# Attention and gated feed-forward on one core: the planner of the attention phase gets other lengths and urgencies, and the instruction order follows

## The chip, the cores and the metric

The kernel runs on one core of one Trainium2 chip. The metric is the device time of one execution in microseconds (us). Three runs of the kernel before gave 1236.25, 1241.36 and 1247.63; their median, 1241.36 us, is the time before.

## What is computed

The reference runs a random-feature attention over 8 batches, 8 heads, 576 tokens and 64 dimensions (128 features), and sends its output through an RMS norm and a gated feed-forward layer:

```
h   = (x*scale) @ omega.T - |x*scale|^2/2         # for q and for k
phi = exp(h - max(h)) / sqrt(128)                 # q_p, k_p
kv  = k_p.T @ v ; z = sum(k_p)                    # per batch and head
x   = (q_p @ kv) / (q_p @ z + 1e-6)               # 4608 tokens x 512
xn  = x / rms(x) * g
out = (silu(xn @ w_gate) * (xn @ w_val)) @ w_out  # 512 -> 1536 -> 512
```

The weights arrive as 64-bit floats and are turned into 32-bit ones on the chip.

## The kernel before

The 4608 tokens are 36 **chunks** of 128 tokens; a pair of batches has 9 chunks, and three chunks make a **block** (12 blocks). The kernel has two phases.

Phase B (`phase_b`) is the rest of the feed-forward layer, written out in a plain loop over blocks. The change doesn't touch it.

Phase A (`phase_a`) is the attention, the norm and a first part of the gated layer (4 of the 12 column tiles for blocks 0 and 1, 8 for the others). It is built as a list of steps. Names in the views: `ink3`, `inq3` are the loads of chunk 3 of k and q (`features`, L302), `pjk3` and `pjq3` its projection on TensorE (8 products into two PSUM banks, pool `psJ` of four), `sq`, `mx`, `hm`, `bi` the VectorE steps to the exponent's bias, `kp3` and `qp3` the exponentials on ScalarE (L360), which give the two banks back. `kvm0` and `kvp1_0` are the products k_p.T @ v (`kv_mid`, L393, and `kv_half`, L430; the last digit is the half of the heads); the batch needs four chunks of k and a middle one. `attend` (L462) does for a chunk c of q: turn (`qt`, TensorE, copied to `qpT` by ScalarE), numerator and denominator (`nu`), division (`rec`, `x`, VectorE), power of the row (`xn`, ScalarE), root (`ss`, GpSimd), scaling (`xn`, VectorE), turn back (`xt`, TensorE), copies `xr` and `xhi` (ScalarE) and `xlo` (GpSimd). When three chunks are there, `gated` (L592) runs the gated tiles: `ff0_3_1` is block 0, column tile 3, value half (0 is the gate half): 12 products of 384 columns each, then `t` (ScalarE), `u` and `h` (VectorE) and a store. `weights` (L210) loads and converts a half tile n of the weights (`f64`, `mag`, `w`, `whi`, `wlo`); tile f of the gated layer needs n = 2f and 2f+1.

Each step is entered with `add` (L71): its engine, a length in us, the steps it comes after, an urgency (`key`; the smallest goes first) and the buffer slots it takes and gives back. `Plan.order` (L75) plays the list through once, when the kernel is built: each engine takes the most urgent step that is ready and has its slots, for the length that was entered, and a step's users become ready `LAT` after its end (loads `LAND` later still; a load's length is its size over `RATE`). Only the order of the steps comes out of it. Each engine then executes its steps strictly in that order, whatever their true lengths are. The urgencies of the first nine chunks of k and q and of the first 16 weight half tiles stand in the table `KEYS`; the later chunks have their number, and the gated tiles come behind all (key 1000 and up), so that they fill what the others leave.

Of the kernel before, what the change touches and what calls it, by code (L numbers as in the profile page):

```python
# [30 lines left out]
EARLY = 4  # L31
FAS = [EARLY] * 2 + [FA] * (NBLK - 2)
KEYS = {
# [3 lines left out]
    "lead": 7.26,  # L37
    "v": 0.11,
    "kv": -0.32,
    "attend": -0.54,  # L40
}
SCALE = float(D) ** -0.25
EPS = 1e-6
# [10 lines left out]
    lo_eng.tensor_tensor(out=lo, in0=raw, in1=hi.bitcast(F32), op=ALU.subtract)  # L54


LAT = 0.25
LAND = 2.2
RATE = 0.26


class Plan:

    def __init__(self, slots):
        self.slots = dict(slots)
        self.items = []

    def add(self, eng, dur, fn, after=(), key=0.0, take=(), give=(), land=0.0):  # L71
        self.items.append((eng, dur, fn, tuple(after), key, tuple(take), tuple(give), land))
# [2 lines left out]
    def order(self):  # L75
        n = len(self.items)
        left = [len(i[3]) for i in self.items]
        users = [[] for _ in range(n)]
        for i, it in enumerate(self.items):
            for d in it[3]:  # L80
                users[d].append(i)
        ready = {}
        slots = self.slots
        events = []
        out = []
        busy = {}
# [8 lines left out]
        while len(out) < n:  # L95
            for eng, queue in ready.items():
                if busy.get(eng, 0.0) > now + 1e-9:
                    continue
                queue.sort()
                for at, (_, i) in enumerate(queue):  # L100
                    _, dur, _, _, _, take, give, land = self.items[i]
                    want = {t: take.count(t) for t in take}
                    if all(slots[t] >= c for t, c in want.items()):
                        for t in take:
                            slots[t] -= 1
                        del queue[at]
                        out.append((now, i))
                        busy[eng] = now + dur
# [3 lines left out]
            assert events, [self.items[i][:2] for q in ready.values() for _, i in q]  # L112
# [11 lines left out]
        return [i for _, i in out]  # L124


def three_pass(nc, out, pairs, start=True, stop=True):
# [45 lines left out]
def phase_a(ctx, tc, ident, g_sb, mhalf, om, qx, kx, va, vmid, wgv, wout, xn_d, h_d, w_d):  # L173
# [36 lines left out]
    def weights(n, key):  # L210
# [6 lines left out]
        t = {}  # L217
# [53 lines left out]
        i = add("ACT", 0.65, size, [i], key, ["mag"])
        i = add("DVE", 0.9, bound, [i], key)
        i = add("DVE", 0.8, top, [i], key, ["w"], ["mag"])
        i = add("DVE", 0.8, low, [i], key, give=["f64"])
        ends = []
        if n >= 2 * EARLY:

# [17 lines left out]
                op=ALU.subtract,  # L295
            )

        i = add("ACT", 0.62, hi, [i], key)
        st["w", f, j] = add("POOL", 1.5, lo, [i], key)
        add("NONE", 0, lambda: None, ends + [st["w", f, j]], give=["w"])  # L300

    def features(tag, c, key):  # L302
# [66 lines left out]
        s = add("ACT", 0.68, square, [i], key)
        s = add("DVE", 0.7, norm, [s], key)  # L370
        p = add("PE", 1.1, project, [i], key, ["psJ", "psJ", tag + "p"])
        add("NONE", 0, lambda: None, [s, p], key, give=["in" + tag])
        m0 = add("DVE", 0.7, lambda: peak(0), [p], key)
        m1 = add("DVE", 0.7, lambda: peak(1), [m0], key)
        b = add("DVE", 0.45, shift, [m1, s], key)
        e = b
        for n in range(4):
            e = add("ACT", 0.82, lambda n=n: exps(n), [e], key - 0.3, give=["psJ"] if n % 2 else [])
# [14 lines left out]
    def kv_mid(pr, key):  # L393
        c = 9 * pr + 4
        done = []

        def heads(h0, n, t):
            if h0 == 0:
                for b in range(2):
                    st["kv", 2 * pr + b] = tile_("kv", [P, H, D + 1], f"kv{2 * pr + b}")  # L400
            t["pt"] = tile_("psM", [P, 3, 2 * (D + 1)], f"kvm{pr}_{h0}")
            for i in range(n):
                nc.tensor.matmul(
                    t["pt"][:, i, :],
                    lhsT=st["kp", c][:, h0 + i, :],
                    rhs=st["v", c][:, h0 + i, :],
                    start=True,
                    stop=True,
                )

        def out(h0, n, t):
            for b in range(2):
                ve.tensor_scalar_mul(
                    st["kv", 2 * pr + b][:, h0 : h0 + n, :],
                    t["pt"][:, :n, b * (D + 1) : (b + 1) * (D + 1)],
                    1.0 / M,
                )

        last = [st["exp", "k", c], st["vload", c]]
        for h0 in (0, 3, 6):  # L420
            n = min(3, H - h0)
            t = {}
            take = ["psM"] + (["kv", "kv"] if h0 == 0 else [])
            give = ["kp", "vm"] if h0 == 6 else []
            m = add("PE", 0.24 * n, lambda a=(h0, n, t): heads(*a), last, key, take, give)
            last = [m]
            done.append(add("DVE", 0.7, lambda a=(h0, n, t): out(*a), [m], key, give=["psM"]))
        st["kvm", pr] = done

    def kv_half(b, half, key):  # L430
# [31 lines left out]
    def attend(c, key):  # L462
# [105 lines left out]
        for half in range(2):  # L568
            i = add("PE", 0.48, lambda h=half: turn(h), turns, key - 0.1,
                    ["psM"] if half else ["psM", "qpT"], ["qp"] if half else [])  # L570
            turns = [i]
            te.append(add("ACT", 0.63, lambda h=half: turned(h), [i], key - 0.4,
                          give=["psM"]))
        for half in range(2):
            after = te[half : half + 1] + [st["kvh", b, half] for _, _, b in spans] + mixed
            give = (["qpT"] + ["kv"] * len(ends)) if half else []
            i = add("PE", 0.92, lambda h=half: mix(h), after, key - 0.2,
                    ["psM"] if half else ["psM", "x"], give)
            mixed = [i]
            nd.append(add("DVE", 0.8, lambda h=half: divide(h), [i], key - 0.3, give=["psM"]))  # L580
        i = add("ACT", 0.9, power, nd, key - 0.5, ["xn"])
        i = add("POOL", 1.0, root, [i], key - 5)
        i = add("DVE", 1.05, scale, [i], key - 0.4, give=["x"])
        i = add("PE", 0.48, xturn, [i], key - 0.3,
                ["psM", "xr"] + (["xT"] if c % NC == 0 else []), ["xn"])
        i = add("ACT", 0.63, xout, [i], key - 0.6, give=["psM"])
        s = add("SP", 0.26 / RATE, xstore, [i], key - 0.3, land=LAND)
        i = add("ACT", 0.65, xhi, [i], key - 0.6)
        st["x", c] = add("POOL", 1.4, xlo, [i], key - 0.3)
        add("NONE", 0, lambda: None, [s, st["x", c]], give=["xr"])  # L590

    def gated(blk, f, key):  # L592
# [34 lines left out]
        top = -1000 + key  # L627
        g = add("PE", 2.09, lambda: ff(0), xs + [st["w", f, 0]], key, ["psF"])
        v = add("PE", 2.09, lambda: ff(1), xs + [st["w", f, 1], g], key, ["psF"],
                ["xT"] if f == FAS[blk] - 1 else [])  # L630
        i = add("ACT", 0.51, gate, [g], top, ["t"])
        i = add("DVE", 0.58, silu, [i], top, ["u"], ["t", "psF"])
        i = add("DVE", 0.58, value, [i, v], top, ["h"], ["u", "psF"])
        add("SP", 0.2 / RATE, store, [i], top, give=["h"], land=LAND)

    nch = NBLK * NC
# [176 lines left out]
```

## Time and profile before

| what | before |
|---|---|
| median of three runs | 1241.36 us |
| the profiled execution | 1247.33 us |
| its span, first to last instruction | 1245.5 us |
| mean granted TensorE clock | 0.965 |
| busy: TensorE, VectorE, ScalarE, GpSimd | 1213.0, 587.7, 509.6, 96.3 us |
| first gated tile starts | 103.09 us |

The profiled execution lies at the slow end of the three runs, 1.83 us lie around its span. In the page, the second part gives the busy share of each engine in 40 slices of some 31 us, and the row PEclk the clock that was granted to TensorE (5 is half speed). A view of windows gives the same for any stretch: for each engine the busy us and the number of instructions, then the clock, the DMA share and GB/s. A timeline gives start, length, engine, line and the operation, and in square brackets the idle time before it with what ended it. Of TensorE's matrix products a float32 one stands as two records: a projection of 8 products is x16, a kv half of 16 products x32.

### The profile page before, as it was taken

The numbers are of one execution on the slowest core, as the hardware profiler recorded it, in microseconds if no ns is written. First come the engines' busy times: TensorE is split into PE (matmuls) and PEld (weight loads), VectorE is DVE, ScalarE is ACT, GpSimd is POOL, SyncE is SP. The second block draws the span as 40 slices with busy tenths as digits, with TensorE's granted clock in tenths as the row PEclk, the third lists the DMA queues.
The fourth block names the chain that finished last, engine by engine and source line by source line (L and its number), as shares of the span: only waits on it lengthen the run. The fifth ranks groups of instructions, "written<-read, shape, count | busy, mean of one in ns | idle before, by whom it ended". The sixth has DMA issues, their size and how long they took to land.

```text
span 1245.5 us, 19324 instructions
## 1 busy us (share of the span) xinstructions
PE 1213.0 (97%) x7552; PEld 1127.2 (91%) x7552; DVE 587.7 (47%) x1236; ACT 509.6 (41%) x1258; POOL 96.3 (8%) x131
## 2 busy tenths in 40 slices
PE   5999899999999999999999999999999999999997
PEld 4889899999999999999999989998988889889886
DVE  5656877887777534544433353123232232232222
ACT  6565676766575434444322352122221222122211
POOL 0121212110101010110110000000000000000000
PEclk7658999999999999999999999999999999999999
DMA  7545666667656312222133352022122212210200
GB/s 273 187 127 173 215 209 188 197 194 228 222 174 210 128 63 92 85 79 68 64 107 107 129 160 102 1 102 81 47 93 85 68 60 77 102 58 18 77 26 26
DMA packets 69515, 146.45 MB, mean 118 GB/s; under 512 B 6192, under 2 KB 36016, under 8 KB 68144
## 3 DMA queue, kind: packets, MB, share of 16 engines
q1 hardware_dynamic: 69200, 144.92, 34.9%
q8 instruction: 59, 0.97, 0.3%
q10 hardware_dynamic: 224, 0.30, 0.1%
q14 instruction: 32, 0.26, 0.1%
HBM read 101.68 MB, written 43.52 MB: 117 GB/s over the span
## 4 chain that ended last, share of the span: by engine, by line
PE 92%; DVE 3%; DMA 3%; ACT 1%; issue 1%; SPq 0%; DVEq 0%; ACTq 0%
PE ff L132 10%; PE ff L133 10%; PE ff L134 10%; PE po L132 8%; PE po L133 8%; PE po L134 8%; PE kvp L440 6%; PE ffB L134 6%; PE ffB L132 6%; PE ffB L133 6%; PE nu L488 5%; PE pjk L331 4%; PE pjq L331 3%; PE qt L477 3%; PE xt L538 1%; DMA graw<-w_scratch 1%
## 5 line engine op out<-in xcount | busy, mean ns | idle before, releaser
L132 PE MATMUL ff<-xhi,whi 128*128 128x384 f32 x704 | 248.6, 353 | 1.6 <-DVE u L613 1.0
L133 PE MATMUL ff<-xlo,whi 128*128 128x384 f32 x704 | 238.3, 338 | 0.0
L134 PE MATMUL ff<-xhi,wlo 128*128 128x384 f32 x704 | 238.1, 338 | 0.0
L132 PE MATMUL po<-ohi,hh 128*128 128x512 f32 x432 | 169.3, 392 | 2.4 <-ACT hh L51 2.3
L133 PE MATMUL po<-olo,hh 128*128 128x512 f32 x432 | 169.0, 391 | 0.0
L134 PE MATMUL po<-ohi,hl 128*128 128x512 f32 x432 | 158.7, 392 | 0.0
L132 PE MATMUL ffB<-xhiB,whiB 128*128 128x384 f32 x448 | 150.3, 336 | 0.7 <-ACT whiB L51 0.7
L134 PE MATMUL ffB<-xhiB,wloB 128*128 128x384 f32 x448 | 150.2, 336 | 0.0
L133 PE MATMUL ffB<-xloB,whiB 128*128 128x384 f32 x448 | 150.0, 335 | 0.0
L132 PEld LDWEIGHTS ff<-xhi,whi 128*128 128x128 f32 x704 | 132.4, 188 | 5.1 <-DVE u L613 1.7
L133 PEld LDWEIGHTS ff<-xlo,whi 128*128 128x128 f32 x704 | 132.6, 188 | 0.0
L134 PEld LDWEIGHTS ff<-xhi,wlo 128*128 128x128 f32 x704 | 132.1, 188 | 0.0
L722 DVE TENSOR_TENSOR h<-s,ffB 128x384 f32<-128x384 f32 x56 | 30.9, 552 | 176.3 <-PE ffB L134 176.3
L360 ACT ACTIVATE qp<-pjq,biq 128x128 f32<-128x128 f32 x288 | 88.8, 376 | 31.7 <-DVE biq L351 31.7
L609 ACT ACTIVATE t<-ff 128x384 f32<-128x384 f32 x88 | 43.5, 494 | 139.2 <-PE ff L134 138.8
L54 DVE TENSOR_TENSOR hl<-hA,hh 128x384 fp32r<-128x384 f32 x88 | 48.0, 556 | 109.6 <-ACT hh L51 87.0
L132 PEld LDWEIGHTS po<-ohi,hh 128*128 128x128 f32 x432 | 81.1, 188 | 18.5 <-ACT hh L51 3.6
L51 ACT CAST hh<-hA 128x384 fp32r<-128x384 f32 x88 | 44.7, 514 | 129.6 <-PE po L133 129.0
L134 PEld LDWEIGHTS po<-ohi,hl 128*128 128x128 f32 x432 | 80.9, 188 | 16.6
L360 ACT ACTIVATE kp<-pjk,bik 128x128 f32<-128x128 f32 x288 | 88.6, 380 | 15.2 <-DVE bik L351 14.5
L133 PEld LDWEIGHTS po<-olo,hh 128*128 128x128 f32 x432 | 81.1, 188 | 14.4
L132 PEld LDWEIGHTS ffB<-xhiB,whiB 128*128 128x128 f32 x448 | 84.1, 188 | 3.4 <-ACT whiB L51 1.2
(69 smaller groups left out, 1731.0 us busy)
## 6 DMA issues: line engine op xcount, KB each, us to landing
ink<-in_kx_dram SPq DMA_DIRECT2D x36, 512.0 KB, 4.0
inq<-in_qx_dram SPq DMA_DIRECT2D x36, 512.0 KB, 3.9
h_scratch<-h SPq DMA_DIRECT2D x88, 192.0 KB, 1.8
hA<-h_scratch SPq DMA_DIRECT2D x10, 1536.0 KB, 6.5
f<-in_wgv_dram SPq DMA_DIRECT2D x24, 512.0 KB, 4.5
xn_scratch<-xr SPq DMA_DIRECT2D x36, 256.0 KB, 2.7
xrB<-xn_scratch SPq DMA_DIRECT2D x12, 768.0 KB, 4.2
out_dram<-o SPq DMA_DIRECT2D x36, 256.0 KB, 2.3
```

Source lines behind the costliest of these rows:

```text
L51: nc.scalar.copy(hi, raw)
L54: lo_eng.tensor_tensor(out=lo, in0=raw, in1=hi.bitcast(F32), op=ALU.subtract)
L132: nc.tensor.matmul(out, lhsT=ah, rhs=bh, start=first, stop=False)
L133: nc.tensor.matmul(out, lhsT=ah, rhs=bl, start=False, stop=False)
L134: nc.tensor.matmul(out, lhsT=al, rhs=bh, start=False, stop=last)
L331: nc.tensor.matmul(t["pts"][i][:, hp, :], lhsT=x[rows, hp, :], rhs=om[rows, :], start=True, stop=True,)
L360: nc.scalar.activation(st[tag + "p", c][:, h, :], t["pts"][h % 2][:, h // 2, :], AF.Exp, bias=t["bi"][:, h : h + 1], scale=SCALE,)
L440: nc.tensor.matmul(t["pt"][:, i, :], lhsT=st["kp", c][:, h, :], rhs=st["v", c][:, h, :], start=(n == 0), stop=(n == 3),)
L477: nc.tensor.transpose(t["pt", half][:, i, :], st["qp", c][:, 4 * half + i, :], ident)
L488: nc.tensor.matmul(pt[lo:hi, i, :], lhsT=t["qpT"][:, h, lo:hi], rhs=st["kv", b][:, h, :], start=True, stop=True,)
L609: nc.scalar.activation(t["t"], t[0], AF.Tanh, scale=0.5)
L722: nc.vector.tensor_tensor(out=h, in0=s, in1=pts[1], op=ALU.mult)
```

## The change

The change touches the planner alone: no step is added or taken out, and buffers, loads and loops stay. It

- replaces `KEYS`: other urgencies for the first nine chunks of k and q and the first 16 weight half tiles, a smaller lead of k over q (6.31 for 7.26), later loads of v (`"v"` 1.3 for 0.11) and later kv products (`"kv"` 0.92 for -0.32);
- replaces the lengths of the steps by others (most a few hundredths shorter; `out` of the middle kv product 0.36 for 0.7, `root` 0.8 for 1.0, `scale` 0.9 for 1.05), `LAT` 0.25 by 0.12 and `RATE` 0.26 by 0.31;
- adds to `Plan` a way to enter idle steps for an engine (`self.idle`) until a step `self.until` has begun. The table `self.idle` stays empty, so that nothing comes of it.

```
-    "k": [-26.0, -14.7, -9.5, -8.2, -5.0, -4.8, -0.4, 0.4, 2.6],
-    "q": [-7.2, -2.2, 1.1, 4.2, 4.9, 5.6, 5.9, 6.1, 7.3],
-    "w": [-0.5, -0.2, 0.1, 1.5, 2.7, 4.7, 6.1, 6.7, 8.6, 9.1, 9.4, 10.2, 14.7, 16.9, 17.2, 21.3],
-    "lead": 7.26,
-    "v": 0.11,
-    "kv": -0.32,
-    "attend": -0.54,
+    "k": [-27.9, -16.1, -10.6, -7.5, -7.0, -6.7, -2.6, 1.0, 2.4],
+    "q": [-10.4, -4.7, 2.6, 3.2, 3.5, 4.0, 4.2, 5.3, 6.3],
+    "w": [1.3, -3.3, 0.7, 2.7, 3.9, 6.1, 7.6, 7.6, 8.1, 6.6, 13.1, 10.2, 31.8, 20.7, 15.1, 32.4],
+    "lead": 6.31,
+    "v": 1.3,
+    "kv": 0.92,
+    "attend": -0.48,
...
-LAT = 0.25
+LAT = 0.12
...
-RATE = 0.26
+RATE = 0.31
...
-            done.append(add("DVE", 0.7, lambda a=(h0, n, t): out(*a), [m], key, give=["psM"]))
+            done.append(add("DVE", 0.36, lambda a=(h0, n, t): out(*a), [m], key, give=["psM"]))
...
+            for eng, (dur, fn) in self.idle.items():
+                if not begun and busy.get(eng, 0.0) <= now + 1e-9:
+                    out.append((now, fn))
```

What this does to the order is seen in three places. The rows leave out those that only repeat the row above with the other bank or another chunk.

The first place is TensorE, from the third chunk's turn back to the first gated tile. Before:

```order
L538 MATMUL xt2_862<-ident_58,xn2_827 128x128 x4
L440 MATMUL kvp1_0_885<-v5_266,kp5_581 128x65
L331 MATMUL pjq4_0_914<-om_67,inq4_462 128x128
L440 MATMUL kvp1_1_929<-v5_266,kp5_581 128x65
L477 MATMUL qt3_0_964<-ident_58,qp3_902 128x128 x4
L331 MATMUL pjk10_0_975<-om_67,ink10_757 128x128
L132 MATMUL ff0_0_0_991<-xhi0_708,whi0_139 128x384
```

And now:

```order
L342 MATMUL pjk9_1_786<-om_67,ink9_669 128x128
L549 MATMUL xt2_830<-ident_58,xn2_802 128x128 x4
L342 MATMUL pjq3_0_858<-om_67,inq3_423 128x128
L451 MATMUL kvp1_0_873<-v5_249,kp5_584 128x65
L143 MATMUL ff0_0_0_913<-xhi0_709,whi0_139 128x384
L451 MATMUL kvp1_1_937<-v5_249,kp5_584 128x65
L488 MATMUL qt3_0_970<-ident_58,qp3_926 128x128 x4
L342 MATMUL pjq4_0_979<-om_67,inq4_464 128x128
L499 MATMUL nu3_0_995<-kv0_432,qpT3_969 128x65 x4
L488 MATMUL qt3_1_1004<-ident_58,qp3_926 128x128 x4
L342 MATMUL pjk10_0_1014<-om_67,ink10_807 128x128
L143 MATMUL ff0_0_1_1037<-xhi0_709,whi0_139 128x384
```

The gate half of the first gated tile has moved ahead of `pjq4`, `kvp1_1`, `qt3_0` and `pjk10`, which now stand between it and its value half `ff0_0_1`, together with `nu3` and `qt3_1`; what stands ahead of `kvp1_0` since the first kv product is the same set of steps in another order.

The second place is ScalarE at the same point: the exponentials of chunk 8 of k, whose banks the projection `pjq3` above takes. Before, that projection took the banks of chunk 9, whose exponentials came ahead:

```order
L360 ACTIVATE kp9_798<-pjk9_1_734,bik9_783 128x128 x2
L514 ACTIVATE xn2_827,ss2_828<-x2_801 128x512
L360 ACTIVATE kp8_840<-pjk8_0_788,bik8_831 128x128 x2
L544 COPY xr2_869<-xt2_862 128x512
L360 ACTIVATE kp8_840<-pjk8_1_789,bik8_831 128x128 x2
```

And now:

```order
L325 ACTIVATE ink8_619<-ink8_619 128x512
L525 ACTIVATE xn2_802,ss2_803<-x2_778 128x512
L371 ACTIVATE kp8_822<-pjk8_0_733,bik8_814 128x128 x4
L555 COPY xr2_837<-xt2_830 128x512
L371 ACTIVATE kp8_822<-pjk8_1_734,bik8_814 128x128 x2
L565 CAST xhi0_709<-xr2_837 128x4x128
```

The two last pairs of exponentials of chunk 8 (one in the rows, one behind `xhi0`) stand behind the copy `xr2`, which waits for the `xt2` of TensorE; the projection `pjq3`, which takes the same banks, now waits for both pairs.

The third place is VectorE between the division of chunk 5 (the last of block 1) and the scaling of that chunk, for which TensorE's `xt5` waits. Before:

```order
L504 TENSOR_TENSOR x5_1434<-nu5_1_1429,rec5_1435 128x256
L348 SCALAR_TENSOR_TENSOR hmq6_1456<-mxq6_1422,sqq6_1025 128x8
L351 SCALAR_TENSOR_TENSOR biq6_1457<-hmq6_1456,sqq6_1025 128x8
L318 TENSOR_REDUCE sqk15_1463<-ink15_1350 128x8
L413 TENSOR_SCALAR kv2_1450<-kvm1_0_1452 128x195
L413 TENSOR_SCALAR kv3_1451<-kvm1_0_1452 128x195
L261 SCALAR_TENSOR_TENSOR w9_1425<-f64_9_1089,w9_1425 128x512
L343 TENSOR_REDUCE mxq7_1493<-pjq7_0_1466 128x4
L526 SCALAR_TENSOR_TENSOR xn5_1460<-x5_1434,ss5_1461,g_sb_63 128x512
```

And now:

```order
L515 TENSOR_TENSOR x5_1381<-nu5_1_1376,rec5_1382 128x256
L354 TENSOR_REDUCE mxk11_1368<-pjk11_1_1340 128x4
L359 SCALAR_TENSOR_TENSOR hmk11_1418<-mxk11_1368,sqk11_903 128x8
L362 SCALAR_TENSOR_TENSOR bik11_1419<-hmk11_1418,sqk11_903 128x8
L242 TENSOR_SCALAR mag11_1397<-mag11_1397 128x512
L250 TENSOR_SCALAR mag11_1397<-mag11_1397 128x512
L354 TENSOR_REDUCE mxq7_1434<-pjq7_0_1405 128x4
L537 SCALAR_TENSOR_TENSOR xn5_1415<-x5_1381,ss5_1416,g_sb_63 128x512
```

Six steps stand between the two instead of seven; the middle kv product `kvm1` of the next batches, whose results `kv2` and `kv3` VectorE copies, has moved behind block 1's gated tiles. On TensorE, `qt6_0`, `pjq7` and `qt6_1` now stand between `nu5_1` and `xt5`. From the last result of block 0's gated tiles (`h0_3`) to the first of block 1's (`u1_0`) VectorE had 50 rows between and now has 34.

More of the change, by code (lines that the diff above doesn't have):

```diff
@@ L69, in __init__ @@
         self.items = []
+        self.idle = {}
+        self.until = None
     def add(self, eng, dur, fn, after=(), key=0.0, take=(), give=(), land=0.0):
@@ L94, in order @@
         now = 0.0
-        while len(out) < n:
+        begun, extra = False, 0
+        while len(out) < n + extra:
             for eng, queue in ready.items():
@@ L107, in order @@
                         out.append((now, i))
+                        begun = begun or i == self.until
                         busy[eng] = now + dur
@@ L111, in order @@
                         break
-            assert events, [self.items[i][:2] for q in ready.values() for _, i in q]
+            for eng, (dur, fn) in self.idle.items():
+                if not begun and busy.get(eng, 0.0) <= now + 1e-9:
+                    out.append((now, fn))
+                    extra += 1
+                    busy[eng] = now + dur
+                    heapq.heappush(events, (now + dur, -2, -1))
+            assert events and extra < n, [self.items[i][:2] for q in ready.values() for _, i in q]
             now = events[0][0]
@@ L123, in order @@
                         come(u)
-        return [i for _, i in out]
+        return [self.items[i][2] if isinstance(i, int) else i for _, i in out]
 def three_pass(nc, out, pairs, start=True, stop=True):
@@ L270, in weights @@
         i = add("SP", 0.52 / RATE, load, key=key, take=["f64"], land=LAND)
[L271 to L274, printed above, removed]
+        i = add("ACT", 0.69, size, [i], key, ["mag"])
+        i = add("DVE", 0.92, bound, [i], key)
+        i = add("DVE", 0.72, top, [i], key, ["w"], ["mag"])
+        i = add("DVE", 0.73, low, [i], key, give=["f64"])
         ends = []
@@ L296, in lo @@
             )
-        i = add("ACT", 0.62, hi, [i], key)
-        st["w", f, j] = add("POOL", 1.5, lo, [i], key)
+        i = add("ACT", 0.63, hi, [i], key)
+        st["w", f, j] = add("POOL", 1.31, lo, [i], key)
         add("NONE", 0, lambda: None, ends + [st["w", f, j]], give=["w"])
@@ L368, in features @@
         i = add("SP", 0.52 / RATE, load, key=key, take=["in" + tag], land=LAND)
[L369 to L370 removed]
+        s = add("ACT", 0.65, square, [i], key)
+        s = add("DVE", 0.69, norm, [s], key)
         p = add("PE", 1.1, project, [i], key, ["psJ", "psJ", tag + "p"])
         add("NONE", 0, lambda: None, [s, p], key, give=["in" + tag])
[L373 to L375 removed]
+        m0 = add("DVE", 0.69, lambda: peak(0), [p], key)
+        m1 = add("DVE", 0.69, lambda: peak(1), [m0], key)
+        b = add("DVE", 0.4, shift, [m1, s], key)
         e = b
         for n in range(4):
[L378 removed]
+            e = add("ACT", 0.76, lambda n=n: exps(n), [e], key - 0.3, give=["psJ"] if n % 2 else [])
         st["exp", tag, c] = e
@@ L571, in attend @@
             turns = [i]
-            te.append(add("ACT", 0.63, lambda h=half: turned(h), [i], key - 0.4,
+            te.append(add("ACT", 0.6, lambda h=half: turned(h), [i], key - 0.4,
                           give=["psM"]))
@@ L579, in attend @@
             mixed = [i]
[L580 to L583, printed above, removed]
+            nd.append(add("DVE", 0.77, lambda h=half: divide(h), [i], key - 0.3, give=["psM"]))
+        i = add("ACT", 0.83, power, nd, key - 0.5, ["xn"])
+        i = add("POOL", 0.8, root, [i], key - 5)
+        i = add("DVE", 0.9, scale, [i], key - 0.4, give=["x"])
         i = add("PE", 0.48, xturn, [i], key - 0.3,
                 ["psM", "xr"] + (["xT"] if c % NC == 0 else []), ["xn"])
-        i = add("ACT", 0.63, xout, [i], key - 0.6, give=["psM"])
+        i = add("ACT", 0.6, xout, [i], key - 0.6, give=["psM"])
         s = add("SP", 0.26 / RATE, xstore, [i], key - 0.3, land=LAND)
-        i = add("ACT", 0.65, xhi, [i], key - 0.6)
-        st["x", c] = add("POOL", 1.4, xlo, [i], key - 0.3)
+        i = add("ACT", 0.63, xhi, [i], key - 0.6)
+        st["x", c] = add("POOL", 1.3, xlo, [i], key - 0.3)
         add("NONE", 0, lambda: None, [s, st["x", c]], give=["xr"])
@@ L627, in gated @@
         top = -1000 + key
+        if plan.until is None:
+            plan.until = len(plan.items)
         g = add("PE", 2.09, lambda: ff(0), xs + [st["w", f, 0]], key, ["psF"])
@@ L630, in gated @@
                 ["xT"] if f == FAS[blk] - 1 else [])
-        i = add("ACT", 0.51, gate, [g], top, ["t"])
-        i = add("DVE", 0.58, silu, [i], top, ["u"], ["t", "psF"])
-        i = add("DVE", 0.58, value, [i, v], top, ["h"], ["u", "psF"])
+        i = add("ACT", 0.5, gate, [g], top, ["t"])
+        i = add("DVE", 0.56, silu, [i], top, ["u"], ["t", "psF"])
+        i = add("DVE", 0.56, value, [i, v], top, ["h"], ["u", "psF"])
         add("SP", 0.2 / RATE, store, [i], top, give=["h"], land=LAND)
@@ L656, in phase_a @@
     with tc.manual_schedule():
-        for i in plan.order():
-            plan.items[i][2]()
+        for begin in plan.order():
+            begin()
 def phase_b(ctx, tc, w_d, xn_d, h_d, out):
```

## The prediction

> **What bounds the kernel now.** The page comes first, then a table of windows cut at TensorE's own steps, then the timeline of TensorE where that table shows a loss.
>
> ```profile
> PE 1213.0 (97%) x7552; PEld 1127.2 (91%) x7552; DVE 587.7 (47%) x1236; ACT 509.6 (41%) x1258; POOL 96.3 (8%) x131
> PEclk7658999999999999999999999999999999999999
> ```
>
> TensorE is the bound: 97% busy. But the clock it was granted is low in the first four slices, some 125 us, and there alone. The table by stage (busy us of each engine, then the clock):
>
> ```profile
> core 0: us, PE busy (x) PEld busy (x) DVE busy (x) ACT busy (x) POOL busy (x), PEclk, DMA share, GB/s
> 0.00:37.70 37.70, 21.92 (x152) 17.98 (x153) 23.73 (x52) 24.95 (x71) 3.14 (x9) 0.77 0.79 262
> 37.70:91.20 53.50, 50.77 (x269) 47.01 (x269) 31.34 (x76) 32.39 (x93) 11.83 (x14) 0.51 0.47 157
> 91.20:103.10 11.90, 11.90 (x70) 11.12 (x69) 5.11 (x12) 2.84 (x9) 0.00 (x0) 0.50 0.30 91
> 130.00:145.00 15.00, 11.02 (x88) 9.69 (x85) 14.25 (x32) 10.40 (x30) 4.85 (x5) 0.89 0.64 198
> 145.00:650.00 505.00, 503.44 (x3811) 485.36 (x3811) 316.99 (x730) 272.47 (x737) 69.81 (x96) 1.00 0.46 149
> ```
>
> From 145 us to the end of the attention phase TensorE is idle for 1.6 of 505 us at full clock. The work there is the same in both kernels, so a new order can win nothing there. What an order can move lies in the first 145 us: up to 37.7 us TensorE waits (15.8 us idle), from there to 103 us it is busy but at half clock, and between 130 and 145 us it is idle for 4.0 us again. That half clock means half speed is seen in the chain of waits, which has the same steps later at full clock,
>
> ```profile
> 106.49 0.44 PE qt L477 x4
> 109.05 0.84 PE nu L488 x8
> 320.25 3.52 PE kvp L440 x32
> 323.77 1.09 PE pjk L331 x16
> ```
>
> against the timeline of TensorE ahead of the first gated tile:
>
> ```profile
> 79.17 0.79 PE L331 MATMUL pjq<-om,inq 64*128 64x128 f32 x2
> 81.43 2.07 PE L331 MATMUL pjq<-om,inq 64*128 64x128 f32 x14 [1.47 <-ACT kp L360]
> 83.44 1.11 PE L538 MATMUL xt<-ident,xn 128*128 128x128 f32 x4
> 84.34 6.93 PE L440 MATMUL kvp<-v,kp 128*128 128x65 f32 x32
> 91.20 2.08 PE L331 MATMUL pjq<-om,inq 64*128 64x128 f32 x16
> 93.21 7.09 PE L440 MATMUL kvp<-v,kp 128*128 128x65 f32 x32
> 100.09 1.06 PE L477 MATMUL qt<-ident,qp 128*128 128x128 f32 x4
> 101.08 2.08 PE L331 MATMUL pjk<-om,ink 64*128 64x128 f32 x16
> 103.09 0.62 PE L132 MATMUL ff<-xhi,whi 128*128 128x384 f32 x1
> ```
>
> A kv half takes 6.9 us here and 3.5 us later. When does the clock rise? Windows around two points:
>
> ```profile
> 45.00:50.00 5.00, 5.00 (x30) 4.78 (x26) 2.71 (x6) 2.36 (x7) 1.28 (x1) 0.50 0.58 201
> 50.00:55.00 5.00, 5.00 (x26) 4.88 (x27) 1.46 (x5) 1.03 (x3) 0.00 (x0) 0.50 0.38 119
> 96.70:100.10 3.40, 3.40 (x18) 3.40 (x18) 0.17 (x1) 0.29 (x2) 0.00 (x0) 0.50 0.05 6
> 100.10:103.50 3.40, 3.40 (x22) 2.85 (x23) 1.50 (x4) 2.15 (x6) 0.00 (x0) 0.50 0.48 153
> 103.50:106.90 3.40, 3.40 (x25) 3.40 (x25) 2.82 (x7) 1.01 (x3) 0.00 (x0) 1.00 0.78 252
> ```
>
> TensorE is fully busy from 45 to 55 us and stays at half clock: that stretch is mostly kv and numerator products, which stream only 65 columns for each 128 columns of weights loaded. The clock is up from 103.5 us on, right behind 3.4 us that held a turn, a projection and the first gated product without a gap. I read this so: what raises the clock is a stretch of some 3.4 us filled with products that stream as many columns as they load or more, and the gated tiles (384 columns) are the surest of these.
>
> **The change, part by part.** Nothing is added or removed, so busy time at full clock is the same. Three places count.
>
> *The first gated tile comes earlier.* Ahead of `ff0_0_0` stood, since the first kv product, the steps up to the end of `kvp1_0` at 91.20 us, and then `pjq4`, `kvp1_1`, `qt3_0`, `pjk10`: 103.09 - 91.20 = 11.9 us at half clock. These four now come behind it. If the clock is up when they run, they take half of that: **-5.95 us**.
>
> *The stretch before it gets longer.* In the rows of VectorE
>
> ```profile
> 79.27 0.16 DVE L502 TENSOR_SCALAR rec<-nu 128x4 f32<-128x4 f32 x1 [1.21 <-PE nu L488]
> 81.81 0.75 DVE L526 SCALAR_TENSOR_TENSOR xn<-x,ss,g_sb 128x512 f32<-128x512 f32 x1
> ```
>
> the scaling of chunk 2 ends 82.56 - 79.2 = 3.4 us after its numerator (end of `nu2_1` at 79.2 us, T). In the new order one projection that stood ahead of T stands behind it, so T comes 2.0 us earlier, at 77.2 us. Then: `pjk9` to 79.2; `xt2` waits for T + 3.4 = 80.6 and ends at 81.6; ScalarE's copy, two pairs of exponentials and the cast between them take about 0.5 us each from start to start,
>
> ```profile
> 118.00 0.59 ACT L544 COPY xr<-xt 128x512 f32<-128x512 f32 x1 [1.25 <-issue]
> 118.48 0.63 ACT L360 ACTIVATE kp<-pjk,bik 128x128 f32<-128x128 f32 x2
> 118.99 0.63 ACT L554 CAST xhi<-xr 128x512 fp32r<-128x512 f32 x1
> ```
>
> with a hand-over some 2.2 us, so that `pjq3` starts at 83.8 and `kvp1_0` at 85.8 instead of 84.3 us: **+1.5 us**. The first gated tile then starts at 85.8 + 6.9 = 92.7 us, 10.4 us earlier than before. If ScalarE's exponentials come before the copy on time it is nothing; if the other two turns back wait as much, +3.
>
> *The first gated tile itself runs at half clock.* At full clock a half tile takes 113.53 - 111.33 = 2.2 us:
>
> ```profile
> 111.33 0.42 PE L132 MATMUL ff<-xhi,whi 128*128 128x384 f32 x1
> 113.53 0.60 PE L477 MATMUL qt<-ident,qp 128*128 128x128 f32 x4
> ```
>
> Before, 0.4 us of it ran at half clock; now, in the middle between two kv halves, all of it does: **+2.1 us**. The rise comes at the end of a 3.4 us window that I take to lie anywhere, so on average 1.7 us of the kv half behind run slow as well: **+0.85 us**.
>
> *Chunk 5 and the end of block 0's gated tiles.* Two waits of TensorE carry the 4.0 us between 130 and 145 us:
>
> ```profile
> PE kvm L403 <- DVE x L504: 1.9, 1, 1.9
> PE xt L538 <- DVE kv L413: 1.7, 1, 1.7
> ```
>
> VectorE is busy for 14.25 of 15 us there: chunk 5's division waits behind its weight steps, and TensorE's queue behind that. VectorE now has 34 rows instead of 50 up to block 1's first tile. From `nu5_1` to `xt5` the same 3.4 us as at T, and about 1 us of VectorE's other rows, make 4.4 us; `qt6_0`, `pjq7`, `qt6_1` cover 0.53 + 1.09 + 0.53, or 2.2 us (0.53 is my estimate from the 0.44 and 0.60 above). Idle 2.2 instead of 4.0 us: **-1.8 us**; ends 0 and -4.
>
> *Costed at nothing.* Up to 37.7 us the same steps stand ahead of the first kv product. Two more loads (0.27 and 0.52 MB, 2.6 us at about 300 GB/s) now go ahead of `ink4`, but the projections wait for ScalarE there:
>
> ```profile
> PE pjk L331 <- ACT kp L360: 4.0, 3, 1.8
> ```
>
> Without that cover, +2.6. From 145 us on the idle time was 1.6 us; the low end is therefore -1.6, and for the high end I take one more stage like that at 130 us, +4.
>
> Sum: -5.95 + 1.5 + 2.1 + 0.85 - 1.8 = **-3.3 us**. Against the profiled execution, 1247.3, that is 1244.0 us; against the median of the three runs, which lies 6 us lower, **1238 us**. The runs of the kernel before differ by 11.4 us, 0.9%, and I think it is the clock's dice that differ: a change of less than 1% is about what a measurement can't tell from none.
>
> **The rivals.**
>
> *The clock rises earlier, near 71 us.* The new order has `qt2_0`, `qt2_1`, `pjk8` in one piece: 4.0 us of products that fill the array. If one window fits in, the clock is up from there: of the 21.3 us to 92.7, some 4.7 are idle, 16.6 become 8.3; the waits behind, which don't shrink, take back 2; the gated tile no longer runs slow, -2.95. Total -3.3 - 6.3 - 2.95 = -12.5: 1229 us. Against it: the like piece `qt1_0`, `qt1_1`, `pjk7` of before didn't raise the clock, and 3.4 us of idle time around `xt2` and `pjq3` would let it fall again. The Trainium skill ("TensorE: Matmul & The Clock Gate", Part 1) states that one busy window of about 3.4 us gives the full clock, which speaks for this rival; but by that rule the clock would have been up at 50 us, and the rows at 45 to 55 us contradict it for busy time alone. Its Part 4 states that transposes don't count as busy, which speaks against it; no run here shows that yet.
>
> *The first gated tile is too short.* It lasts 4.3 us at half clock and stands between two kv halves. If no window is filled, the clock stays down until `ff0_0_1`, which three more half tiles make certain. `kvp1_1`, `qt3_0`, `pjq4`, `nu3_0`, `qt3_1`, `pjk10`, `nu3_1` take at half clock 6.9 + 1.0 + 2.0 + 1.7 + 1.0 + 2.0 + 1.7 = 16.3 us, 8.2 too much; with 1.7 for the window in the gated tiles instead of 0.85 it is +9.0: -3.3 + 9.0 = +5.7, 1247 us, slower than before. It decides whether at 97 us the granted clock is still half.
>
> *VectorE falls behind after it and the clock falls again.* Between `u0_0` and block 1, weight half tile 9, which isn't needed until block 2, is now converted before 6 and 7. If the stage loses another 4.0 us idle and two windows (6.8 us) at half clock, 3.4 us, on top of the rival above: +13.1, 1254 us, slower by 1%.
>
> *The order changes nothing that sets the end*, as from 145 us on; that is inside the forecast's range.
>
> **How the numbers follow.** The forecast gets 0.50, the early rise 0.18, the short tile 0.20, the fall 0.12. The likeliest is 1238 us, its own range 1231 to 1245. The early rise and the fall reach to 1229 and 1254 with unknown ends beyond, so 1226 to 1253 leaves out about 2 in 10. Faster by over 1% (below 1229) is the early rise and a tail of the forecast, 0.21; slower by over 1% (above 1254) half of the fall and some of the bounds, 0.11; within 1%: 0.68.
>
> **What would show it.** In the profile after: the first `ff` at 92 to 94 us, an idle time of about 2 us ahead of the `pjq` behind the third `xt`; granted clock full from about 97 us; less idle time at chunk 5. A clock up at 75 us, or still half at 115 us, or a first `ff` later than 97 us would make it wrong, and so would a loss of more than 4 us behind 145 us.

## The result, and the profile after

The changed kernel takes 1248.54 us (median of 20 runs, 1245.73 to 1250.17), the kernel before 1236.64 us in as many runs beside it (1227.58 to 1247.63). The ratio is 1.009, 95% interval 1.0069 to 1.011: slower, by some 12 us, where the prediction had a gain of 3. The profiled execution after took 1248.85 us, its span is 1247.1 us.

The page of after shows engine totals and the clock:

```profile
PE 1199.9 (96%) x7552; PEld 1113.7 (89%) x7552; DVE 591.0 (47%) x1236; ACT 509.4 (41%) x1258; POOL 97.4 (8%) x131
PEclk9969999999999999999998999999999999999999
```

TensorE is busy for 13 us less than in the profiled execution before, because its clock was full for longer (from 37.7 to 91.2 us it is 0.81 on the mean, and 0.51 in the table of the prediction), and yet the span is no shorter: the time has become idle time. The table by stage of after says where:

```profile
core 0: us, PE busy (x) PEld busy (x) DVE busy (x) ACT busy (x) POOL busy (x), PEclk, DMA share, GB/s
37.70:91.20 53.50, 45.23 (x356) 41.92 (x358) 39.04 (x92) 35.42 (x98) 13.30 (x14) 0.81 0.54 179
130.00:145.00 15.00, 15.00 (x131) 14.01 (x130) 10.31 (x25) 11.66 (x31) 4.19 (x5) 1.00 0.45 143
145.00:400.00 255.00, 244.85 (x1947) 231.44 (x1946) 195.20 (x447) 161.40 (x460) 33.10 (x42) 0.98 0.62 201
400.00:650.00 250.00, 250.00 (x1750) 244.13 (x1749) 112.56 (x258) 100.31 (x251) 32.33 (x48) 1.00 0.26 84
650.00:750.00 100.00, 94.46 (x500) 90.59 (x499) 41.36 (x66) 32.19 (x56) 0.00 (x0) 0.97 0.37 121
```

and the same stages of before:

```profile
145.00:400.00 255.00, 253.44 (x2050) 240.94 (x2050) 199.77 (x458) 168.68 (x471) 37.29 (x48) 1.00 0.66 209
650.00:750.00 100.00, 97.92 (x536) 93.86 (x535) 42.51 (x69) 34.02 (x60) 1.29 (x1) 1.00 0.38 125
```

Between 145 and 400 us TensorE is idle for 10.2 us (before: 1.6), between 650 and 750 us for 5.5 (before: 2.1), and in both its clock is below full. The waits of TensorE name the steps, first from 145 to 645 us, then from 645 to 760:

```profile
PE ff L143 <- DVE u L624: 5.1, 4, 2.0
PE xt L549 <- DVE xn L537: 2.8, 2, 1.9
```

```profile
PE ff L143 <- DVE u L624: 4.2, 1, 4.2
```

The step `u` gives back the PSUM bank of a gate half; the gated tiles have two banks, so the next half waits for it.

**The wait at 184 us.** The timelines of the four engines, after:

```profile
178.87 1.67 POOL L568 TENSOR_TENSOR xlo<-xr,xhi 128x512 fp32r<-128x512 f32 x1 [3.94 <-DVE x L515]
179.43 1.67 DVE L272 SCALAR_TENSOR_TENSOR w<-f,w 128x512 int32<-128x512 int32 x1
181.56 0.50 ACT L620 ACTIVATE t<-ff 128x384 f32<-128x384 f32 x1
182.69 0.16 DVE L513 TENSOR_SCALAR rec<-nu 128x4 f32<-128x4 f32 x1 [0.35 <-PE nu L499]
183.44 0.68 DVE L354 TENSOR_REDUCE mxk<-pjk 128x4 f32<-128x512 f32 x1
184.04 0.54 DVE L624 SCALAR_TENSOR_TENSOR u<-t,ff 128x384 f32<-128x384 f32 x1
184.64 0.44 PE L143 MATMUL ff<-xhi,whi 128*128 128x384 f32 x1 [1.98 <-DVE u L624]
```

`t` is done at 182.06 us, but `u` starts at 184.04: in VectorE's queue a division (`rec`, `x`) and a maximum (`mxk`) stand ahead of it, and the division waits for TensorE's `nu`. `w`, entered with 0.73 us, took 1.67 beside GpSimd's `xlo`, but that isn't what made the wait: VectorE had caught up and stood idle for 0.35 us ahead of the division, and in `a_mid` (below), where this wait is gone, the same step is as slow:

```profile
179.73 1.66 DVE L278 SCALAR_TENSOR_TENSOR w<-f,w 128x512 int32<-128x512 int32 x1
```

The wait is in the plan itself. The urgencies of the division of chunk 10 (9.22) and of the maximum of chunk 16 of k (9.69) go ahead of that of `u2_1` (17), so `Plan.order` puts them first and then keeps TensorE idle for 2.27 us in its own play-through.

**The wait at 657 us.** ScalarE, VectorE and TensorE at the end of the attention phase, after:

```profile
651.99 2.85 ACT L51 CAST xhiB<-xrB 128x1536 fp32r<-128x1536 f32 x2 [3.74 <-DMA xn_scratch<-xr]
653.51 3.43 DVE L54 TENSOR_TENSOR xloB<-xrB,xhiB 128x1536 fp32r<-128x1536 f32 x2 [3.86 <-ACT xhiB L51]
654.75 0.86 ACT L620 ACTIVATE t<-ff 128x384 f32<-128x384 f32 x2
656.85 1.01 DVE L624 SCALAR_TENSOR_TENSOR u<-t,ff 128x384 f32<-128x384 f32 x2
657.45 0.69 PE L143 MATMUL ff<-xhi,whi 128*128 128x384 f32 x1 [4.16 <-DVE u L624]
658.58 0.52 PE L143 MATMUL ff<-xhi,whi 128*128 128x384 f32 x1
```

and before, at the same place:

```profile
656.40 2.86 ACT L51 CAST xhiB<-xrB 128x1536 fp32r<-128x1536 f32 x2 [1.91 <-DMA xn_scratch<-xr]
661.86 0.45 PE L132 MATMUL ff<-xhi,whi 128*128 128x384 f32 x1 [0.21 <-DVE u L613]
```

Phase B's first two splittings of xn stand ahead of `t10_4` and `u10_4`. In the order before, `t10_4` still came ahead of them, since the gated tiles were paired otherwise (1 with 2, 3 with 4; now 2 with 3, 4 with 5), and TensorE waited 0.21 us. After its wait of 4.16 us the products take 0.52 us where they take 0.34 at full clock, for some 6 us; the clock had gone to half in the wait, for 6.8 us in all.

**The first 100 us.** TensorE up to the first gated tile, after:

```profile
61.28 0.63 PE L549 MATMUL xt<-ident,xn 128*128 128x128 f32 x4 [1.53 <-DVE xn L537]
68.19 1.09 PE L549 MATMUL xt<-ident,xn 128*128 128x128 f32 x4 [1.73 <-DVE xn L537]
71.56 2.07 PE L342 MATMUL pjq<-om,inq 64*128 64x128 f32 x14 [1.56 <-ACT kp L371]
73.56 7.09 PE L451 MATMUL kvp<-v,kp 128*128 128x65 f32 x32
80.41 0.67 PE L143 MATMUL ff<-xhi,whi 128*128 128x384 f32 x1
83.51 0.34 PE L144 MATMUL ff<-xlo,whi 128*128 128x384 f32 x1
```

The clock had been full from 35.4 us on, fell behind the first of these stalls, at 62.7 us, and came back inside the first gated tile: a kv half of 7.09 us, a first product of 0.67, and the last ones of 0.34.

### The profile page after: what moved, and what is told of

Same layout as the page of the kernel before. It is cut to its first block, busy times and chain, and to the rows that moved or that the text cites. A ratio compares the mean times of both kernels' runs of the same rounds, so it can differ in the third digit from the quotient of the medians.

```text
span 1247.1 us, 19335 instructions
## 1 busy us (share of the span) xinstructions
PE 1199.9 (96%) x7552; PEld 1113.7 (89%) x7552; DVE 591.0 (47%) x1236; ACT 509.4 (41%) x1258; POOL 97.4 (8%) x131
## 5 line engine op out<-in xcount | busy, mean ns | idle before, releaser
L143 PE MATMUL ff<-xhi,whi 128*128 128x384 f32 x704 | 251.4, 357 | 9.3 <-DVE u L624 9.3
L144 PE MATMUL ff<-xlo,whi 128*128 128x384 f32 x704 | 241.4, 343 | 0.0
L145 PE MATMUL ff<-xhi,wlo 128*128 128x384 f32 x704 | 241.3, 343 | 0.0
L143 PEld LDWEIGHTS ff<-xhi,whi 128*128 128x128 f32 x704 | 134.9, 192 | 13.1 <-DVE u L624 10.4
L371 ACT ACTIVATE qp<-pjq,biq 128x128 f32<-128x128 f32 x288 | 88.2, 374 | 10.9 <-DVE biq L362 10.8
L624 DVE SCALAR_TENSOR_TENSOR u<-t,ff 128x384 f32<-128x384 f32 x88 | 48.4, 551 | 88.7 <-ACT t L620 88.7
```

What stands on the lines that cost most here:

```text
L143: nc.tensor.matmul(out, lhsT=ah, rhs=bh, start=first, stop=False)
L144: nc.tensor.matmul(out, lhsT=ah, rhs=bl, start=False, stop=False)
L145: nc.tensor.matmul(out, lhsT=al, rhs=bh, start=False, stop=last)
L371: nc.scalar.activation(st[tag + "p", c][:, h, :], t["pts"][h % 2][:, h // 2, :], AF.Exp, bias=t["bi"][:, h : h + 1], scale=SCALE,)
L624: ve.scalar_tensor_tensor(out=t["u"], in0=t["t"], scalar=1.0, in1=t[0], op0=ALU.add, op1=ALU.mult)
```

## The experiments

Five theories were on record first. P: the 4.2 us wait at the end of the attention phase and the half clock behind it are the loss. K: the new urgencies cost time in the middle. C: the early gain is real, but other waits take it up. L: the shorter hand-over `LAT` makes orders that wait. W: the kernel before loses some 10 us on the mean to half clock ahead of its first gated tiles, after little. Each ratio below is to the kernel before, timed on the same chip.

**Another execution of the kernel before** (`b_again`, no edit).

> The kernel before once more, for a second profile. Theory P (the end of the attention phase): whatever the clock does in the first 100 us, no wait of more than 0.5 us on VectorE between 650 and 665 us, and idle time of TensorE between 145 and 650 us under 4 us. Theory C (an early clock only uncovers the other engines, whatever the order): if the clock is up earlier than 103 us in this execution, the idle time between 145 and 650 us grows towards the 10 us of the changed kernel and the time stays near 1247 us. By P an earlier clock makes it shorter, 1228 to 1240 us.

It took 1227.62 us, 19.7 less than the profiled execution that the prediction read, with the same instructions. The clock's row of its page, then its TensorE up to the first gated tile:

```profile
PEclk9989999999999999999999999999999999999999
```

```profile
73.41 4.03 PE L440 MATMUL kvp<-v,kp 128*128 128x65 f32 x32
77.37 1.16 PE L331 MATMUL pjq<-om,inq 64*128 64x128 f32 x16
78.47 3.79 PE L440 MATMUL kvp<-v,kp 128*128 128x65 f32 x32
83.72 0.44 PE L132 MATMUL ff<-xhi,whi 128*128 128x384 f32 x1
```

The kv halves ahead of the first gated tile take 4.03 and 3.79 us, nearly all at full clock. That tile starts at 83.72 us, not at 103.09; the two executions are 19.4 us apart there and 19.7 at the end. From 145 to 650 us `b_again` is idle for 3.6 us and it has no wait for VectorE near 655 us, as theory P expected; theory C, by which the earlier clock would uncover some 10 us of waits there, fell. Over 75 executions of before in which it was recorded, the granted clock runs from 0.967 to 0.997, the time from 1222.32 to 1249.57 (median 1235), and the two correlate at -0.83. So the profile that the prediction started from was near the bad end, 65 us at half clock from 38.7 us on. `b_again` is near the good end; the median clock of the 75, 0.983, lies between the two (0.965 and 0.992). In most executions of before a part of the early gain was therefore there already.

**One half of the change alone** (`b_keys`: new `KEYS`, old lengths; `b_len`: old `KEYS`, new lengths, `LAT`, `RATE`), **and the last pairs shifted** (`a_shift`):

```
+        lone = [st["v", 10, 2]] if (blk, f) == (10, 3) else []
-        g = add("PE", 2.09, lambda: ff(0), xs + [st["w", f, 0]], key, ["psF"])
+        g = add("PE", 2.09, lambda: ff(0), xs + [st["w", f, 0]] + lone, key, ["psF"])
+        st["v", blk, f] = v
```

> The new urgencies with the old lengths, LAT and RATE. Its last gated tiles go in the pairs of before. Theory P: no wait over 0.5 us near 655 us, ratio to before 0.995 to 1.003. Theory K: 8 to 12 us idle between 145 and 400 us as in the changed kernel, ratio 1.006 to 1.010.

> The old urgencies with the new lengths, LAT and RATE. Its last gated tiles go in the pairs of the changed kernel. Theory P: the wait of 4.2 us near 655 us is there, 5 to 8 us slower than before, ratio 1.004 to 1.007. Theory K: idle time between 145 and 400 us stays under 4 us and the ratio near 1.000.

> The changed kernel with one more dependency: the gate half of tile 3 of block 10 comes after the value half of tile 2, which shifts the pairs in which the last gated tiles go by one, as they were before. Theory P: the 4.2 us wait of TensorE near 655 us goes, and with it 6.8 us at half clock (3.4 us): 7.6 us less than the changed kernel, ratio to before about 1.003. Theory K (the new urgencies cost the time in the middle of the attention phase, 145 to 400 us): the time stays within 2 us of the changed kernel, ratio 1.009.

`b_keys` 1239.49 us (1.0052, 1.0014 to 1.009), `b_len` 1247.28 (1.012, 1.0092 to 1.0148), `a_shift` 1244.84 (1.0108, 1.0076 to 1.0141). `b_len` has after's pairs and a 3.8 us wait at the end, `b_keys` before's pairs and no such wait. The middle is lost in both: 145 to 400 us `b_keys` is idle for 7.1 us, `b_len` for 4.9. `a_shift` kept a wait of 2.1 us and no half clock; in its order tile 4 goes with tile 2 and tile 3 comes behind them, so these aren't quite the pairs of before. Its gain is not clear: 3.7 us below after, but the ratio is no lower than that of after, 1.009. Neither theory's ranges held in all three. P has its mechanism, but it is not the whole; K holds, but is not due to the urgencies alone.

**`LAT` alone** (`a_lat`: after with 0.25; `b_lat`: before with 0.12):

> The changed kernel with one number put back: LAT 0.25 for 0.12 (the hand-over time that the planner adds after each step). Its last gated tiles go in the pairs of before again. Theory L (the shorter hand-over makes orders that wait in the middle too, since a step is put where its input is only just ready): the 4.2 us wait near 655 us goes and the idle time between 145 and 400 us falls from 10 to under 5 us: 1234 to 1240 us, ratio to before 0.998 to 1.003. Theory K (the urgencies and the other lengths make the waits in the middle): only the end is mended, 1240 to 1245 us, ratio 1.003 to 1.007, and 8 us or more stay idle between 145 and 400 us.

> The kernel before with LAT 0.12 for 0.25 and nothing else. Theory L: the wait of about 4 us near 655 us, and more idle time between 145 and 400 us than the 1.6 us of before; ratio to before 1.006 to 1.011. Theory K: the wait at the end alone, ratio 1.003 to 1.006.

`a_lat` 1256.13 us (1.0166, 1.0117 to 1.0215), `b_lat` 1264.13 (1.0244, 1.0201 to 1.0286). Each direction made it slower, outside what either theory expected, so L fell. `LAT` does decide the pairs (`a_lat` has before's, `b_lat` after's), but each new number lays the middle out anew: from 145 to 400 us `a_lat` is idle for 10.8 us, `b_lat` for 12.3.

The plan says most of this before any run. Played through for each kernel's list with the entered lengths, `Plan.order` has TensorE idle, from 145 to 400 us of its own time, for

| | before | `b_len` | after | `b_keys` | `a_lat` | `b_lat` |
|---|---|---|---|---|---|---|
| planned, us | 8.3 | 11.8 | 16.7 | 17.5 | 20.6 | 25.3 |
| measured, us | 1.6 | 4.9 | 10.2 | 7.1 | 10.8 | 12.3 |

The sizes are too large, but the order is right but for after and `b_keys`, and between before and after the plan has 8.4 us more where the traces have 8.6.

**TensorE kept busy wherever the plan has it idle** (`b_warm`, `a_warm`: ahead of the first gated tile, products of the identity with itself, read by nobody, entered as the idle step of TensorE):

```
+    def fill():
+        if not warm:
+            warm["t"] = tile_("psF", [P, TB], "warm")
+        for _ in range(2):
+            nc.tensor.matmul(warm["t"][:, 0:P], lhsT=ident, rhs=ident, start=True, stop=True)
+    plan.idle["PE"] = (0.27, fill)
```

> The kernel before with products of the identity with itself, into a PSUM bank that is otherwise empty, put into the order wherever the planner has TensorE idle ahead of the first gated tile (extra work, no result uses it). Theory W (before loses on the mean some 10 us to half clock between 38 and 103 us, differently in each execution): the clock is full from 20 us to the end, the runs lie within 5 us of each other, near 1227 us, ratio 0.990 to 0.995. Rival: what sets that stretch is ScalarE and VectorE, and the fillers stand in the way: ratio 1.00 or above with the clock full.

> The same fillers in the changed kernel. Theory W: it has the full clock before 62 us in most executions already and loses 20 us of half clock after that, some 8 us: it comes down to 1238 to 1242 us, with the waits in the middle and the 4.2 us at the end as they were. Rival (the waits in the middle swallow what the clock gives): it stays within 2 us of the changed kernel's 1248.

`b_warm` 1292.88 us (1.0475, 1.0428 to 1.0523), `a_warm` 1260.57 (1.0219, 1.0177 to 1.0262). The mean clock of the profiled executions was 0.996 and 0.998, but the fillers stand in a strict queue: the first `t` came at 126 and 121 us, 40 us later than in `b_again` and 37 later than in after. So the rival on record for `b_warm` came about: full clock, and the fillers in the way. As a test of W and of what the clock is worth this says nothing; it shows what a filler in the wrong place costs.

**The losses taken out one by one.** `a_mid` keeps after's order but for three steps `u`, which go ahead of what they stood behind; `a_end` gives phase B's first two splittings to GpSimd; `a_fix` is both.

```
+    plan.moves = [
+        (st["u", 2, 1], st["nd", 10, 1]),
+        (st["u", 2, 4], st["m0", "k20"]),
+        (st["u", 4, 1], st["nd", 18, 1]),
+    ]
```

`Plan.order` puts the first step of each pair ahead of the second when it has laid out the order (`nd` is the division of chunks 10 and 18, `m0` the maximum of chunk 20 of k). And for `a_end`:

```
+        if blk < 2:
+            nc.gpsimd.tensor_copy(xhi, raw)
+            nc.gpsimd.tensor_tensor(out=xlo, in0=raw, in1=xhi.bitcast(F32), op=ALU.subtract)
+        else:
             split(nc, xhi, xlo, raw, nc.scalar, nc.vector)
```

> The changed kernel with its planned order kept, except that three steps u of gated tiles (u2_1, u2_4, u4_1) are put ahead of the division or maximum that they stood behind in VectorE's queue; nothing else is moved and nothing is left out. Theory M (strict queues: the two TensorE waits of 1.98 us for u near 184.6 and 222.8 us, the one of 0.84 near 341 us and the two windows of 3.4 us at half clock behind them are real losses of the new order): these waits fall below 0.5 us each and the clock does not fall there, so 4.0 us of idle time and up to 3.4 us of half clock go: 1241 to 1245 us, 3.5 to 7.5 below the changed kernel's 1248.5, ratio to before 1.003 to 1.007. Theory N (such a wait is only moved to the next place where TensorE waits for the steps now behind u): the same 1248.5, ratio 1.009, with waits of about 2 us for xt, pjk or nu right behind those places.

> The changed kernel, except that the splitting of xn for the first two blocks of the last phase (xhiB0, xhiB1, xloB0, xloB1) runs on GpSimd, which is idle there, in place of ScalarE and VectorE; the gated tiles keep their new pairs. Theory P (the 4.16 us wait near 657 us and the 6.8 us at half clock behind it come from the two long steps of the last phase that stand ahead of t10_4 on ScalarE and u10_4 on VectorE): no wait over 0.5 us between 645 and 700 us, no fall of the clock there, 5.5 to 7.6 us less: 1241 to 1243 us, ratio to before 1.003 to 1.006. Rival G (GpSimd slows VectorE's steps beside it, as it did from 0.68 to 1.67 us in the middle, and ends so late that the last phase's first tile waits): u and h take over 1 us for some 15 us, TensorE waits 2 to 5 us there or at the start of the last phase near 703 us, and the time stays at 1247 to 1250 us.

> Both edits at once in the changed kernel: the three steps u put ahead, and the first two splittings of the last phase on GpSimd. If the two losses are separate and make up what the new order loses (theories M and P): the sum of the two gains, 9 to 15 us below the changed kernel's 1248.5, 1233.5 to 1239.5 us, ratio to before 0.998 to 1.003, so no longer slower than before. If they hang together or only move elsewhere (N, G): 1245 us or more, ratio 1.007 or more.

`a_mid` 1241.82 us (1.005, 1.0028 to 1.0072): 6.7 below after. Two windows at the first of the three places, of after,

```profile
181.00:184.60 3.60, 1.65 (x20) 1.39 (x16) 3.18 (x9) 3.12 (x11) 1.36 (x2) 1.00 0.66 236
184.60:188.40 3.80, 3.76 (x16) 3.33 (x18) 2.12 (x5) 2.14 (x7) 0.67 (x2) 0.63 0.44 174
```

and of `a_mid`:

```profile
181.00:184.60 3.60, 3.40 (x32) 3.14 (x31) 3.50 (x9) 3.10 (x10) 1.13 (x1) 1.00 0.67 204
184.60:188.40 3.80, 3.80 (x34) 3.42 (x33) 3.51 (x8) 3.72 (x13) 0.91 (x3) 1.00 0.69 240
```

TensorE is busy through nearly all of both, and the clock, 0.63 in the second window of after, stays full. The wait at 222.8 us went in the same way; at the third place 1.00 us stayed, now for `h` in place of `u`. So theory N (the wait only moves on) fell at the two long waits and held at the short one.

`a_end` 1242.57 us (1.0071, 1.0046 to 1.0097): 6.0 below after. Its GpSimd and VectorE at the place:

```profile
649.99 2.88 POOL L713 CAST xhiB<-xrB 128x1536 fp32r<-128x1536 f32 x2 [2.64 <-DMA h_scratch<-h]
652.84 6.96 POOL L714 TENSOR_TENSOR xloB<-xrB,xhiB 128x1536 fp32r<-128x1536 f32 x2
653.18 0.55 DVE L630 SCALAR_TENSOR_TENSOR h<-u,ff 128x384 f32<-128x384 f32 x1 [1.04 <-PE ff L145]
657.95 0.55 DVE L624 SCALAR_TENSOR_TENSOR u<-t,ff 128x384 f32<-128x384 f32 x1 [2.09 <-ACT t L620]
```

`u` and `h` keep their 0.55 us beside GpSimd, and TensorE is busy for 103.96 of the 105 us from 645 us on. Rival G fell.

`a_fix` 1236.28 us (1.0017, 0.9995 to 1.0038): 12.3 below after, against 6.7 + 6.0 for the two edits apart, and no longer distinguishable from before. After was timed in another session, and its ratio to before gives smaller gains (0.4, 0.2 and 0.7% for the three). The three kernels shared a session, and there the splittings add 5.5 us to `a_mid` and the steps `u` add 6.3 to `a_end`: the two losses are separate, some 6 us each. They are the two largest, but not all. In the middle `a_fix` is still idle for 7.2 us, where before has 1.6:

```profile
145.00:400.00 255.00, 247.82 (x1992) 234.59 (x1992) 197.61 (x451) 163.05 (x463) 34.57 (x44) 0.99 0.62 202
```

**What became of the early gain.** `a_fix`, like the profiles of after, `a_shift`, `a_mid` and `a_end`, shows the clock falling at the stalls between 60 and 72 us. `a_best` adds identity products at these three stalls only:

```
+    plan.fills = [
+        (lambda: fill(8), st["xt", 1]),
+        (lambda: fill(14), st["xt", 2]),
+        (lambda: fill(8), st["p", "q3"]),
+    ]
```

> The kernel with both edits (steps u ahead, first splittings of the last phase on GpSimd), and in addition TensorE products of the identity with itself, whose results nobody reads, ahead of the three stalls before the first gated tile: 8 ahead of the second xt, 14 ahead of the third, 8 ahead of the pjq that follows; the transposes, projections and all other work are unchanged. In the profiles of the new order TensorE waits there 1.5, 1.7 to 2.7 and 1.6 us, and its clock is at half for 13.7 to 20.5 us behind them, until about 83 us. Theory S (the early gain of the new order is lost to this half clock behind the stalls that it made): the clock stays full from 50 us on, the kvp stretch and the first gated tile take half as long, first ff at 74 to 77 us, and the time falls by 6 to 10 us against the kernel with both edits: 1226 to 1231 us, ratio to before 0.992 to 0.997, faster than both kernels. Theory C (the early clock only uncovers other waits, or the added products delay the chain by as much as they save): 1235 to 1240 us, ratio 1.000 to 1.004, with as much idle time ahead of the next xt or pjq between 77 and 110 us.

`a_best` takes 1231.01 us (1229.14 to 1233.87), 0.9964 of before (0.994 to 0.9989): faster than both kernels, and 5.3 us below `a_fix` (in another session), just short of the 6 to 10 us that theory S expected. The windows, `a_fix` first, then `a_best`:

```profile
58.50:62.00 3.50, 1.83 (x21) 1.53 (x22) 1.61 (x3) 2.74 (x9) 1.10 (x3) 1.00 0.23 70
65.40:72.00 6.60, 2.41 (x12) 1.81 (x13) 6.46 (x16) 5.45 (x17) 1.98 (x4) 0.67 0.60 199
72.00:80.00 8.00, 8.00 (x43) 7.78 (x42) 4.58 (x8) 4.66 (x14) 3.23 (x3) 0.50 0.75 227
```

```profile
65.40:72.00 6.60, 6.52 (x62) 6.08 (x60) 6.46 (x15) 5.45 (x18) 2.31 (x2) 1.00 0.66 210
72.00:80.00 8.00, 8.00 (x67) 8.00 (x67) 5.28 (x11) 6.18 (x19) 2.55 (x2) 1.00 0.69 223
```

and `a_best`'s first gated product:

```profile
75.20 0.42 PE L152 MATMUL ff<-xhi,whi 128*128 128x384 f32 x1
```

From 72 to 80 us TensorE gets through 43 records at half clock and 67 at full; the first gated tile starts at 75.20 us instead of 80.25. So theory C fell: the early clock is worth its time, and the changed kernel loses it to the half clock behind the stalls, 13.7 to 20.5 us of it in the profiles named. This is not the new order's alone: `b_again` is at half clock for 13.7 us between 57 and 74 us, behind stalls of its own. The same few products in the order of before were not tried, so `a_best` doesn't show that the new order is the better one. `a_best` is still idle for 7.3 us between 145 and 400 us, which is left to win.

## Why the prediction was wrong

- **The range.** 1248.54 us lies inside the 1226 to 1253 of the prediction, but by luck: its high end stood for a fall of the clock ahead of block 1, which didn't come.
- **The sum was made against one execution, at its clock.** The prediction named the clock's dice as the spread of the runs, and yet took the median as the profiled time less 6 us, with all terms unchanged. The term that carried the sign, -5.95, halves four steps that ran at half clock in that profile. In `b_again` the kv halves there take 4.03 and 3.79 us instead of 6.93 and 7.09: in such an execution of before there was next to nothing of it to win, and in the median one a part. After has its first gated tile at 80.41 us against 83.72 in `b_again`, 3.3 us earlier, not 10.4. That this is far ahead of the 92 to 94 us of the forecast is no merit of the moved steps: the clock of this execution was full from 35.4 to 62.7 us, ahead of them.
- **The stalls ahead of it (+1.5).** Forecast as a wait for the third `xt` and one ahead of `pjq`; they came, 1.73 and 1.56 us. Before has its share of them (1.54 and 1.47 us in `b_again`). Their price was wrong: the half clock that they bring was used only as an argument against the early rise, and `a_best` against `a_fix` measures 5.3 us for it behind the three stalls.
- **The first gated tile at half clock, and where the clock comes back (+2.1, +0.85).** Right in kind: the clock is back at 83 us, 2.6 us into `ff0_0_0`, and the rival of the tile that is too short did not come about.
- **Chunk 5 (-1.8).** Right: the whole idle time from 103 to 145 us is 1.8 us instead of 4.0, of it 1.69 ahead of `xt5`, where 2.2 were forecast. Against `b_again` (2.6 in the same stretch) it is worth 0.8.
- **"Costed at nothing", from 145 us on (low -1.6, high +4).** This step failed, and it decided the sign. It took the 1.6 us of idle time before for a property of the work, "a new order can win nothing there", and forgot that it can lose. The new order makes TensorE idle for 10.2 us from 145 to 400 us and for 4.16 at the last pairs, with half clock behind the longer waits; putting the largest of these waits right gives back some 6 us in the middle (`a_mid`) and some 6 at the end (`a_end`). The sign that the prediction named, "a loss of more than 4 us behind 145 us", is what the trace shows.
- **The rivals.** All looked at the first 145 us. The order of the last pairs against phase B's splittings could be read from the two orders before the run, and the waits in the middle from the planner's own play-through, 16.7 us of idle TensorE instead of 8.3; neither was.

That before's order runs the middle nearly without waits is what the trace of before showed and no more: the four other orders tried from there on (`b_keys`, `b_len`, `a_lat`, `b_lat`) were idle for 4.9 to 12.3 us between 145 and 400 us. In the plan, too, it has the fewest. Why the true waits are so much shorter than the planned ones is open. Open too is what decides, in one and the same kernel, whether the clock falls at 38 us or not.

## What to carry to other kernels

When a change lays an order out anew, price the stretches that are tight now as what can be lost, not as what can't be won; look in the new order for what stands ahead of the step that gives a buffer back, and ask the planner for the idle time that its own play-through has. Take a second profile of the kernel before when its runs spread by 1%, and make the sum against the one whose clock is usual. A stall of 1.5 to 2 us on TensorE can cost its own length and half clock behind it (at 184.6 us 1.98 us and 3.4 us of half clock; the 2.1 us of `a_shift` had none behind it). A few products that nobody reads, put at three such stalls alone, took back 5.3 us here; put at every planned gap they lost 12 us and more.

## What the runs showed of the hardware

- **A VectorE step beside GpSimd.** `w` took 1.67 us at 179.43 beside GpSimd's `xlo` (the like step at 178.71, which had started ahead of `xlo`, took 0.68), while `u` and `h`, which read one operand from PSUM, kept 0.55 beside 6.96 us of GpSimd subtractions. The Trainium skill ("SBUF — State Buffer", "Who interferes with whom") states that a VectorE instruction with two SBUF inputs contends with a GpSimd instruction that reads SBUF, and that one with at most one, outside the 2-port modes, does not. These rows agree; the planner has no such entry, though this slow step made no wait of TensorE.
- **The clock falls at stalls well below 3 us and does not come back with busy time alone.** After: 1.65 us busy of 3.6 from 181.00 us on, and the clock is at half for 3.4 us from 185.5 on. In `a_fix` TensorE is fully busy from 72 to 80 us at 0.50. In `a_best` the same kv products run there at 1.00, once the clock is up. The Trainium skill ("TensorE: Matmul & The Clock Gate", Part 1) gives about 3.4 us of idle time for the fall and as much of busy time for the rise; here less idle time was enough for the one, and more busy time not enough for the other.
